# An expert layer's helper work: a gate's exponential later in ScalarE's queue, raw words loaded two parts ahead, all scaled output copies on ScalarE

## Chip, cores and metric

One core of a Trainium2 chip runs the whole program. The metric is device time in microseconds (us), from the median of three runs; lower is better.

## What is computed

Three layers follow one another: a gated recurrent attention (4 x 8 heads, 768 steps, 40 wide), a top-1 mixture of 8 experts over 3072 tokens of width 320, and a dense layer with a rational activation. The change lies in the second and in the preparation of the third:

```
logits = xn @ en.T / tau
expert_idx = argmax(logits); probs = softmax(logits)
gate_w = probs[token, expert_idx]
for e in range(8):
    h = maximum(x[mask] @ w1[e], 0)
    out[mask] = gate_w[mask, None] * (h @ w2[e])
...
h = x @ w_in                     # third layer, 320 -> 2048
g = P(h) / Q(h); return g @ w_out
```

`w_in` and `w_out` are handed over as raw 8-byte words, which the kernel turns into pairs of fp32 parts (a high and a low one).

## The kernel before

Every fp32 product is made of three products of shorter operands: each matrix is split into a high part (`h1`, `h2`, `hh`, `xh`) and a remainder (`l1`, `l2`, `hl`, `xl`). ScalarE writes the high part, VectorE or GpSimd the remainder by a subtraction.

The expert stage is a hand-ordered loop of 64 blocks `n`, eight (`fb` 0 to 7) for each of eight experts `e`. The order in which the loop writes instructions is the order of every engine's queue. A block does the following.

- `gemm1(n)` multiplies 128 columns of `w1[e]` with the expert's tokens (TensorE, L228, into one of two banks `ph`); ScalarE writes `hh` (L1454) and VectorE `hl` (L1455). A bank is free again, for block n+2, when `hl` has been read from it.
- `gemm2(n - 2)` multiplies `hh` and `hl` with `w2` (TensorE, L1469 to L1471) into the banks `yb0` to `yb3`, one for each 128 tokens, over the eight blocks of the expert. After the last of them `y_store` copies every bank, times the gate of its token, to `ysb`: banks 0 and 2 on ScalarE (L1487), 1 and 3 on VectorE (L1483). GpSimd writes the row numbers (L1478) and sends each part out with an indirect DMA (`y_scatter`, L129). The next expert's first `gemm2` writes the same banks and so waits for these copies.
- `w_hi` and `w_lo` split the weights of an expert that comes later: one ScalarE copy (L183 in even blocks, L185 in odd ones), and two GpSimd subtractions (L192 or L196).
- `x_prep` (blocks `fb` 4 to 6) transposes the next expert's tokens; `x_load` (`fb` 0) fetches the tokens of the expert after that with indirect DMAs on GpSimd (L1421).
- Two generators are stepped in turn. `gates` makes the gates of the next expert, started in its predecessor's last block, four steps to a block: 17 small VectorE steps (a maximum L1049, a square root L1773 to L1784, a difference L1052, L1054, a reciprocal, a product L1058), then the exponential on ScalarE (L1060), then three VectorE steps (L1062 to L1066). `dbl` turns the raw words of the third layer into high and low parts: 32 parts of eight steps each, an absolute value on ScalarE (`ct`, L1371), six steps on VectorE (L1373 to L1391), and a copy to `winh` (L1394) or two stores to DRAM (L1397, L1398). Six of its steps fall into a block of the experts 1 to 4, three from expert 5 on.

`dbl_load(i)` (L1347) fetches the raw words of part i with DMAs in SyncE's queue (L1351, L1352 or L1355). Its tile `raw` has two buffers, and part i + 1 is fetched after the first step of part i. The same queue carries the experts' weights (L162 to L168) and the stores of the `dbl` parts.

The third layer's first steps (`s3_step`) are interleaved with the last five blocks, so the stage ends gradually.

Of the kernel before, what the change touches and what calls it, by code (L numbers as in the profile page):

```python
# [11 lines left out]
I32 = mybir.dt.int32  # L12
U32 = mybir.dt.uint32
AF = mybir.ActivationFunctionType
ALU = mybir.AluOpType
# [6 lines left out]
def kernel(  # L22
# [17 lines left out]
    nc = tc.nc  # L40
    B, HD, S = qT.shape
    NT, DM = out.shape
    NE, _, FE = w1.shape
# [52 lines left out]
    head = const.tile([128, NE * JS, XI], F32, name="head")  # L96
# [944 lines left out]
    nc.vector.tensor_reduce(out=midl, in_=mall, axis=AX.X, op=ALU.add)  # L1041
    nc.vector.tensor_copy(xid[:, 1:, :], midl[:, 1:, :])

    def gates(pool, g, hd, tag):

        n = g.shape[1]
        sq, lg = hd[:, :, 0], hd[:, :, 1:]
        nrm, ta, tb, mx = (pool.tile([128, n], F32, name=v + tag, bufs=1) for v in ("nrm", "ta", "tb", "mx"))
        nc.vector.tensor_reduce(out=mx, in_=lg, axis=AX.X, op=ALU.max)  # L1049
        yield  # L1050
        yield from sqrt_steps(nc, nrm, sq, ta, tb)
        nc.vector.tensor_tensor(out=lg, in0=lg, in1=mx.unsqueeze(2).broadcast_to([128, n, NE]), op=ALU.subtract)  # L1052
        yield
        nc.vector.tensor_scalar(out=nrm, in0=nrm, scalar1=1e-6, scalar2=None, op0=ALU.add)  # L1054
        yield
        nc.vector.reciprocal(out=nrm, in_=nrm)
        yield
        nc.vector.tensor_tensor(out=lg, in0=lg, in1=nrm.unsqueeze(2).broadcast_to([128, n, NE]), op=ALU.mult)  # L1058
        yield
        nc.scalar.activation(out=lg, in_=lg, func=AF.Exp)  # L1060
        yield
        nc.vector.tensor_reduce(out=g, in_=lg, axis=AX.X, op=ALU.add)  # L1062
        yield
        nc.vector.tensor_scalar(out=g, in0=g, scalar1=1e-9, scalar2=None, op0=ALU.add)
        yield
        nc.vector.reciprocal(out=g, in_=g)  # L1066
        yield
# [265 lines left out]
    with ExitStack() as mctx:  # L1333
# [9 lines left out]


        def dbl_load(i):
            raw = mp.tile([128, 3 * 128, 2], I32, name="raw", bufs=2)
            if i < 16:  # L1347
                cs = slice(i * 128, (i + 1) * 128)
                rv = raw.rearrange("p (k f) t -> p k f t", k=3)
                for k in range(2):  # L1350
                    nc.sync.dma_start(out=rv[:, k], in_=win32[k * 128:(k + 1) * 128, cs, :])  # L1351
                    nc.sync.dma_start(out=rv[64 * k:64 * k + 64, 2], in_=win32[256:320, cs, :])  # L1352
            else:
                f0 = (i - 16) * 128
                nc.sync.dma_start(  # L1355
                    out=raw[:, 0:DM, :].rearrange("p f t -> p (f t)"), in_=wout32[f0:f0 + 128, :]
                )
            sx["raw", i] = raw
# [42 lines left out]
        def dbl():  # L1401
            for i in range(ND):
                for k, _ in enumerate(dbl_split(i)):
                    if k == 0 and i + 1 < ND:
                        dbl_load(i + 1)
                    yield

        def slots(k):
# [66 lines left out]
        def y_store(e, js):  # L1475
            j0, j1 = js[0], js[-1] + 1
            ysb = mp.tile([128, 4, YR], F32, name="ysb", bufs=1)
            nc.gpsimd.tensor_copy(ysb[:, j0:j1, 0].bitcast(I32), xid[:, e, j0:j1])  # L1478
            for j in js:
                r = rows(e, j)  # L1480
                gj = gate[:r, JS * e + j:JS * e + j + 1]
                if j % 2:
                    nc.vector.tensor_scalar(  # L1483
                        out=ysb[:r, j, 1:], in0=sr["yb"][j][:r, 0:DM], scalar1=gj, scalar2=None, op0=ALU.mult
                    )
                else:
                    nc.scalar.activation(out=ysb[:r, j, 1:], in_=sr["yb"][j][:r, 0:DM], func=AF.Copy, scale=gj)  # L1487
                if e < NE - 1:
                    y_scatter(e, j, ysb)
            sx["ysb"] = ysb  # L1490
# [46 lines left out]
                x_prep(0, kk, (*phs, pt0)[kk][:, NP:])  # L1537

        coef_load()
        dbl_load(0)  # L1540
        dbls = dbl()

        with tc.tile_pool(name="ov", bufs=1) as ov, tc.tile_pool(name="ovp", bufs=1, space=PSUM) as ovp:
# [104 lines left out]
        for n in range(NB + LAG2):  # L1648
            e, fb = divmod(n, NFB)
            qq, half = divmod(n, 2)  # L1650
            if n < NB:
                gemm1(n)
            if n >= LAG2:
                gemm2(n - LAG2)

            if n == NB - 12:
                y_load(0)
            for kk in range(3):
                if n == XPN[kk]:
                    x_prep(NE, kk)  # L1660
            if n == S3N[0]:
                banks(tctx, "h", 3)
            if n == NB:
                banks(hctx, "s", 2, side="right")
                sr["S"] = sr["s"].rearrange("p a b -> p (a b)")[:, 0:2 * TG].rearrange("p (a b) -> p a b", a=2)
            if n in S3N:
                s3_step(S3N.index(n))
            for p, at in enumerate((NB - 6, NB - 6, NB - 4, NB - 2, NB, NB + 1)):
                if n == at:
                    wout_load(p)  # L1670
            if n >= NB:
                continue
            if half == 0 and 5 < qq + 4 < 4 * NE:
                w_load(qq + 4)
            if fb == 0 and 1 < e + 1 < NE:
                x_load(e + 1)
            if n == 5:
                y_store(0, range(NP // 128))
            if n == 2:

                b4 = [v.unsqueeze(2).broadcast_to([128, NE, JS]) for v in (within, start)]
                t4 = mp.tile([128, NE, JS], F32, name="t4", bufs=1)
                nc.vector.tensor_tensor(out=t4, in0=slot, in1=b4[0], op=ALU.is_ge)
                nc.vector.scalar_tensor_tensor(
                    out=t4, in0=t4, scalar=2.0**20, in1=slot, op0=ALU.mult, op1=ALU.add
                )
                nc.vector.tensor_tensor(out=yrow, in0=t4, in1=b4[1], op=ALU.add)
            if 4 <= fb <= 6 and e + 1 < NE:
                x_prep(e + 1, fb - 4)
            if 3 < qq + 3 < 4 * NE:  # L1690
                w_hi(qq + 3, half)
                for i in range(2):
                    w_lo(qq + 3, 2 * half + i, nc.vector if half and n < 10 else nc.gpsimd)


            if n == 1 or fb == NFB - 1 and e + 1 < NE:
                g = 0 if n == 1 else e + 1
                gs = slice(g * JS, g * JS + slots(g).stop)
                gsteps = gates(mp, gate[:, gs], head[:, gs, :], "g")
            a, b, c = (W0 * min(max(v - NFB, 0), 4 * NFB) + W1 * max(min(v, DE) - 5 * NFB, 0) for v in (n, n + 1, NB))  # L1700
            nd, ng = b * ND * NS // c - a * ND * NS // c, (4 if n > 5 else 6) if n else 0
            for i in range(max(nd, ng)):
                if i < ng:
                    next(gsteps, None)
                if i < nd:
                    next(dbls)
# [128 lines left out]
```

## Time and profile before

| | |
|---|---|
| median of 3 runs | 845.56 us (842.04 to 846.34) |
| the profiled execution | 845.91 us |
| its span, first to last instruction | 844.2 us |
| busy over the span: TensorE / VectorE / ScalarE / GpSimd | 91% / 89% / 58% / 71% |
| instructions: VectorE, ScalarE | 1421, 839 |
| the expert loop | from about 225 us to about 475 us |

Busy time is what an engine's instructions take from start to end, so an instruction that is held up after its start counts as busy. A wait is idle time before an instruction, put down to what ended it. In the tables PE is TensorE, DVE VectorE, ACT ScalarE, POOL GpSimd and SPq the queue of SyncE.

### The profile page before, as it was taken

The numbers are of one execution on the slowest core, as the hardware profiler recorded it, in microseconds if no ns is written. First come the engines' busy times: TensorE is split into PE (matmuls) and PEld (weight loads), VectorE is DVE, ScalarE is ACT, GpSimd is POOL, SyncE is SP. The second block draws the span as 40 slices with busy tenths as digits, with TensorE's granted clock in tenths as the row PEclk, the third lists the DMA queues.
The fourth block names the chain that finished last, engine by engine and source line by source line (L and its number), as shares of the span: only waits on it lengthen the run. The fifth ranks groups of instructions, "written<-read, shape, count | busy, mean of one in ns | idle before, by whom it ended". The sixth has DMA issues, their size and how long they took to land.

```text
span 844.2 us, 14447 instructions
## 1 busy us (share of the span) xinstructions
PE 769.7 (91%) x4724; PEld 712.9 (84%) x4724; DVE 749.7 (89%) x1421; ACT 488.6 (58%) x839; POOL 595.4 (71%) x595
## 2 busy tenths in 40 slices
PE   8988988978798897988889899999999999999994
PEld 5877776768787777888789799999999999999993
DVE  7999999998589999999898988888889888988882
ACT  5243333333346454434544887878787877787772
POOL 6654343464565857767874578998989898989883
PEclk6899999998999999999999999999999999999998
DMA  8998788643465656577677303000101010000000
GB/s 207 257 241 236 224 238 223 195 130 98 130 190 161 197 158 197 171 217 218 192 223 223 102 16 110 17 32 16 32 15 33 9 40 9 17 1 24 1 24 24
DMA packets 86964, 102.41 MB, mean 121 GB/s; under 512 B 7915, under 2 KB 79219, under 8 KB 86880
## 3 DMA queue, kind: packets, MB, share of 16 engines
q1 hardware_dynamic: 82976, 88.63, 36.9%
q0 software_dynamic: 3904, 12.77, 4.7%
q8 instruction: 39, 0.64, 0.3%
q14 instruction: 45, 0.37, 0.2%
HBM read 84.01 MB, written 17.93 MB: 121 GB/s over the span
## 4 chain that ended last, share of the span: by engine, by line
PE 47%; DVE 12%; DMA 4%; issue 3%; ACT 3%; POOL 2%; SPq 1%; POOLq 0%; ACTq 0%; DVEq 0%
PE h L228 20%; PE yb L1300 6%; PE yb L1298 6%; PE yb L1299 6%; PE ph L228 4%; DMA r<-in_w 2%; DVE hl L1455 2%; DMA raw<-in_w_out 2%; DVE head L1058 1%; DVE nrmg L1784 1%; PE yb L1469 1%; PE yb L1470 1%; PE yb L1471 1%; PE h L1101 1%; DVE ct L1375 1%
## 5 line engine op out<-in xcount | busy, mean ns | idle before, releaser
L1238 POOL TENSOR_TENSOR U<-U,A 128x768 f32<-128x768 f32 (+1 forms) x65 | 119.3, 1835 | 28.6 <-ACT U L1230 23.9
L1300 PE MATMUL yb<-wo,gl 128*128 128x320 f32 x384 | 119.5, 311 | 1.8 <-POOL gl L1284 1.8
L1284 POOL TENSOR_TENSOR gl<-P,gh 128x768 fp32r<-128x768 f32 x63 | 117.8, 1870 | 3.7 <-ACT gh L1281 3.0
L1298 PE MATMUL yb<-wo,gh 128*128 128x320 f32 x384 | 119.2, 310 | 1.2 <-ACT gh L1281 1.2
L1299 PE MATMUL yb<-wo,gh 128*128 128x320 f32 x384 | 119.0, 310 | 0.0
L192 POOL TENSOR_TENSOR l<-r,h 128x384 fp32r<-128x384 f32 x64 | 67.1, 1072 | 56.5 <-ACT h L183 48.3
L1214 ACT ACTIVATE P<-h,coef 128x768 f32<-128x768 f32 (+1 forms) x65 | 64.0, 985 | 72.0 <-PE h L228 72.0
L228 PE MATMUL h<-xh,winh 128*128 128x384 f32 x256 | 90.5, 353 | 3.9 <-DVE P L1247 3.8
L228 PE MATMUL h<-xh,winl 128*128 128x384 f32 x256 | 86.6, 338 | 0.0
L228 PE MATMUL h<-xl,winh 128*128 128x384 f32 x256 | 86.4, 338 | 0.0
L1242 DVE TENSOR_TENSOR P<-P,h 128x768 f32<-128x768 f32 (+1 forms) x65 | 61.2, 941 | 27.8 <-ACT A L1222 23.1
L1469 PE MATMUL yb<-h,hh 128*128 128x320 f32 (+1 forms) x216 | 69.1, 320 | 10.1 <-DVE ysb L1483 8.5
L228 PE MATMUL ph<-xh,h 128*128 128x256 f32 (+4 forms) x152 | 56.2, 370 | 21.2 <-DVE hl L1455 16.9
L1300 PEld LDWEIGHTS yb<-wo,gl 128*128 128x128 f32 x384 | 72.5, 189 | 2.6 <-POOL gl L1284 2.6
L1298 PEld LDWEIGHTS yb<-wo,gh 128*128 128x128 f32 x384 | 72.6, 189 | 1.5 <-ACT gh L1281 1.5
L1299 PEld LDWEIGHTS yb<-wo,gh 128*128 128x128 f32 x384 | 72.5, 189 | 0.0
L1232 POOL TENSOR_SCALAR U<-A,coef 128x768 f32<-128x768 f32 x56 | 55.1, 984 | 21.3 <-ACT A L1222 20.8
L1470 PE MATMUL yb<-l,hh 128*128 128x320 f32 (+1 forms) x216 | 68.1, 315 | 0.0
L1471 PE MATMUL yb<-h,hl 128*128 128x320 f32 (+1 forms) x216 | 68.0, 315 | 0.0
L1247 DVE SCALAR_TENSOR_TENSOR P<-P,coef,h 128x768 f32<-128x768 f32 (+1 forms) x65 | 65.2, 1003 | 2.3
L1273 DVE SCALAR_TENSOR_TENSOR P<-P,coef,s 128x768 f32<-128x768 f32 (+1 forms) x62 | 62.0, 1000 | 1.7
L1265 DVE SCALAR_TENSOR_TENSOR U<-U,s 128x768 f32<-128x768 f32 (+1 forms) x62 | 58.0, 935 | 4.4 <-ACT s L1261 4.3
(693 smaller groups left out, 2386.2 us busy)
## 6 DMA issues: line engine op xcount, KB each, us to landing
fb<-fz_d SPq DMA_DIRECT2D x22, 512.0 KB
r<-in_w SPq DMA_DIRECT2D x32, 320.0 KB
r<-in_w SPq DMA_DIRECT2D x32, 256.0 KB
raw<-in_w_out SPq DMA_DIRECT2D x16, 320.0 KB
r<-in_w SPq DMA_DIRECT2D x64, 64.0 KB
raw<-in_w_in SPq DMA_DIRECT2D x32, 128.0 KB
x_rows<-xt SPq DMA_DIRECT2D x24, 164.5 KB
xt<-y_sorted SPq DMA_DIRECT2D x8, 481.5 KB
```

Of the source, the lines that this page charges most:

```text
L192: eng.tensor_tensor(out=l1[:, :, sl], in0=r1[:, :, sl], in1=h1[:, :, sl].bitcast(F32), op=ALU.subtract)
L228: mms = [nc.tensor.matmul(ps, lhsT=a, rhs=b, start=(i == 0), stop=(i == 7)) for i, (a, b) in enumerate(seq)]
L1214: r = nc.scalar.activation(out=part("P", m, i), in_=part("ph", m, i), func=AF.Identity, scale=coef[:, 3:4], bias=coef[:, 2:3])
L1238: eng.tensor_tensor(out=U, in0=U, in1=part("A", m, i), op=ALU.mult)
L1247: r = nc.vector.scalar_tensor_tensor(out=P, in0=P, scalar=coef[:, 1:2], in1=part("ph", m, i), op0=ALU.add, op1=ALU.mult)
L1284: eng.tensor_tensor(out=part("gl", m, i), in0=part("P", m, i), in1=part("gh", m, i).bitcast(F32), op=ALU.subtract)
L1298: nc.tensor.matmul(y, lhsT=gh[:, i, t], rhs=wh, start=first, stop=False)
L1299: nc.tensor.matmul(y, lhsT=gh[:, i, t], rhs=wl, start=False, stop=False)
L1300: nc.tensor.matmul(y, lhsT=gl[:, i, t], rhs=wh, start=False, stop=last)
L1469: nc.tensor.matmul(y, lhsT=hh[:, js], rhs=h2[:, half, :], start=(fb == 0), stop=False)
L1470: nc.tensor.matmul(y, lhsT=hh[:, js], rhs=l2[:, half, :], start=False, stop=False)
L1471: nc.tensor.matmul(y, lhsT=hl[:, js], rhs=h2[:, half, :], start=False, stop=(fb == NFB - 1))
```

## The change

Three edits. `gates` takes a number of extra turns before the exponential: four for the gates of experts 1 to 7, none for expert 0. `raw` gets a third buffer, parts 0 and 1 are fetched at the start, and the first step of part i is followed by the fetch of part i + 2. In `y_store` ScalarE makes all the scaled copies.

```diff
-    def gates(pool, g, hd, tag):
+    def gates(pool, g, hd, tag, turns=0):
...
         nc.vector.tensor_tensor(out=lg, in0=lg, in1=nrm.unsqueeze(2).broadcast_to([128, n, NE]), op=ALU.mult)
-        yield
+
+        for _ in range(1 + turns):
+            yield
         nc.scalar.activation(out=lg, in_=lg, func=AF.Exp)
...
-            raw = mp.tile([128, 3 * 128, 2], I32, name="raw", bufs=2)
+            raw = mp.tile([128, 3 * 128, 2], I32, name="raw", bufs=3)
...
-                    if k == 0 and i + 1 < ND:
-                        dbl_load(i + 1)
+                    if k == 0 and i + 2 < ND:
+                        dbl_load(i + 2)
...
-                if j % 2:
-                    nc.vector.tensor_scalar(
-                        out=ysb[:r, j, 1:], in0=sr["yb"][j][:r, 0:DM], scalar1=gj, scalar2=None, op0=ALU.mult
-                    )
-                else:
-                    nc.scalar.activation(out=ysb[:r, j, 1:], in_=sr["yb"][j][:r, 0:DM], func=AF.Copy, scale=gj)
+                nc.scalar.activation(out=ysb[:r, j, 1:], in_=sr["yb"][j][:r, 0:DM], func=AF.Copy, scale=gj)
...
-        dbl_load(0)
+        for i in range(2):
+            dbl_load(i)
...
-                gsteps = gates(mp, gate[:, gs], head[:, gs, :], "g")
+                gsteps = gates(mp, gate[:, gs], head[:, gs, :], "g", 4 if g else 0)
```

ScalarE's queue where expert 4's outputs are copied (`y_store`) and on to the exponential of the gates of expert 6, before; lines of the changed kernel are up to three off (L1060 there is L1062, L1487 is L1484).

```order
L1454 ACTIVATE hh_6337<-ph1_119 128x384
L1487 ACTIVATE ysb_6353<-yb0_113,gate_85 128x320
L1487 ACTIVATE ysb_6353<-yb2_4256,gate_85 128x320
L185 ACTIVATE h2_6309<-r2_6187 128x640
L1454 ACTIVATE hh_6389<-ph0_118 128x384
L183 ACTIVATE h1_6408<-r1_6292 128x768
L1454 ACTIVATE hh_6431<-ph1_119 128x384
L185 ACTIVATE h2_6409<-r2_6296 128x640
L1060 ACTIVATE head_84<-head_84 128x3x8
L1371 ACTIVATE ct_6451<-raw_6326 128x320
L1454 ACTIVATE hh_6468<-ph0_118 128x384
```

Now, the same place:

```order
L1456 ACTIVATE hh_6339<-ph1_119 128x384
L1484 ACTIVATE ysb_6355<-yb0_113,gate_85 128x320
L1484 ACTIVATE ysb_6355<-yb1_114,gate_85 128x320
L1484 ACTIVATE ysb_6355<-yb2_4261,gate_85 128x320
L1484 ACTIVATE ysb_6355<-yb3_4265,gate_85 64x320
L185 ACTIVATE h2_6311<-r2_6189 128x640
L1456 ACTIVATE hh_6391<-ph0_118 128x384
L183 ACTIVATE h1_6410<-r1_6294 128x768
L1456 ACTIVATE hh_6433<-ph1_119 128x384
L185 ACTIVATE h2_6411<-r2_6298 128x640
L1373 ACTIVATE ct_6452<-raw_6250 128x320
L1456 ACTIVATE hh_6467<-ph0_118 128x384
```

Two copies have become four, and the exponential is gone from its place between a weight copy (L185) and an absolute value. It stands one block later in the changed queue:

```order
L1456 ACTIVATE hh_6467<-ph0_118 128x384
L1098 ACTIVATE xt4_6300<-xt4_6300 128x3x64
L1079 ACTIVATE xh0_6491<-pt_6486 128x352
L183 ACTIVATE h1_6495<-r1_6404 128x768
L1062 ACTIVATE head_84<-head_84 128x3x8
L1456 ACTIVATE hh_6516<-ph1_119 128x384
```

So one `hh`, one token copy and one weight copy of an even block (L183) now come ahead of it; the `hh` and the weight copy of the next block still come behind.

SyncE's queue in expert 4, at the end of two parts of `w_out` (`ct` and `lo3` are the parts that are stored, `raw` the words that are fetched), before:

```order
L1397 DMA wouth_d_2550<-ct_5810 128x320
L1398 DMA woutl_d_2551<-lo3_5882 128x320
L1355 DMA raw_5892<-in_w_out 128x640
L1397 DMA wouth_d_2550<-ct_5888 128x320
L1398 DMA woutl_d_2551<-lo3_5948 128x320
L1355 DMA raw_5957<-in_w_out 128x640
```

Now:

```order
L1399 DMA wouth_d_2550<-ct_5812 128x320
L1400 DMA woutl_d_2551<-lo3_5884 128x320
L1357 DMA raw_5894<-in_w_out 128x640
L1399 DMA wouth_d_2550<-ct_5890 128x320
L1400 DMA woutl_d_2551<-lo3_5950 128x320
L1357 DMA raw_5959<-in_w_out 128x640
```

The places of loads and stores are the same. What a load brings has moved: `raw_5957` before is read two parts after the one that is stored ahead of it, `raw_5959` now three parts after.

## Rows read from the trace of the kernel before

**Rows 1.** The page's first line.
```profile
span 844.2 us, 14447 instructions
```

**Rows 2.** Busy time by stretch: microseconds from the span's start, length, then each engine.
```profile
core 0: us, PE busy (x) PEld busy (x) DVE busy (x) ACT busy (x) POOL busy (x), PEclk, DMA share, GB/s
...
255.00:455.00 200.00, 175.16 (x996) 161.10 (x997) 190.63 (x385) 94.50 (x189) 141.53 (x148) 0.97 0.64 191
455.00:475.00 20.00, 20.00 (x126) 19.69 (x124) 15.00 (x25) 14.44 (x20) 4.85 (x3) 1.00 0.67 207
```

**Rows 3.** Waits of VectorE from 255 to 455 us: total, times, longest.
```profile
DVE ct L1373 <- ACT ct L1371: 3.6, 5, 1.5
DVE hl L1455 <- ACT hh L1454: 2.4, 3, 1.3
DVE gate L1062 <- ACT head L1060: 0.7, 2, 0.4
DVE xr L1082 <- ACT xr L1077: 0.6, 2, 0.4
```

**Rows 4.** Waits of ScalarE from 225 to 475 us.
```profile
ACT head L1060 <- DVE head L1058: 36.7, 8, 6.2
ACT ct L1371 <- DMA raw<-in_w_out: 21.3, 9, 5.1
...
ACT ct L1371 <- DMA raw<-in_w_in: 14.3, 7, 6.6
```

**Rows 5.** Waits of TensorE from 225 to 475 us.
```profile
PE ph L228 <- DVE hl L1455: 16.9, 14, 2.8
PE yb L1469 <- DVE ysb L1483: 8.5, 4, 3.0
```

**Rows 6.** The line of VectorE's scaled copies: nanoseconds least, median, most.
```profile
L1483 DVE TENSOR_SCALAR ysb<-yb,gate x13: 531/541/546, 237.8 to 475.0; 128x320 f32<-128x320 f32 x11, 64x320 f32<-64x320 f32 x2
```

**Rows 7.** The line of ScalarE's scaled copies.
```profile
L1487 ACT ACTIVATE ysb<-yb,gate x16: 512/524/530, 237.6 to 475.8; 128x320 f32<-128x320 f32 x14, 96x320 f32<-96x320 f32 x2
```

**Rows 8.** Timeline from 289 us: start, length, instruction, idle before and its releaser.
```profile
289.43 0.97 POOL L129 DMA_INDIRECT y_sorted<-ysb,yrow  x1 [0.30 <-DMA raw<-in_w_in]
...
289.99 5.82 DVE L1052 TENSOR_TENSOR head<-head,mxg 128x32 f32<-128x32 f32 x1
...
290.43 1.73 POOL L196 TENSOR_TENSOR l<-r,h 128x320 fp32r<-128x320 f32 x2
...
292.11 1.98 POOL L192 TENSOR_TENSOR l<-r,h 128x384 fp32r<-128x384 f32 x2
...
294.06 1.70 POOL L196 TENSOR_TENSOR l<-r,h 128x320 fp32r<-128x320 f32 x2
...
297.92 0.50 PE L228 MATMUL ph<-xh,h 128*128 128x512 f32 x1 [1.92 <-DVE hl L1455]
...
298.05 0.23 ACT L1060 ACTIVATE head<-head 128x32 f32<-128x32 f32 x1 [5.51 <-DVE head L1058]
```

**Rows 9.** The chain that ended last, merged: start, length, what.
```profile
425.41 5.25 DVE head L1058
```

**Rows 10.** Timeline of VectorE from 406 us.
```profile
406.70 1.15 DVE L1378 TENSOR_SCALAR st__6452<-raw 128x320 int32<-128x320 int32 x1
407.88 1.19 DVE L1380 SCALAR_TENSOR_TENSOR vt<-raw,st__6452 128x320 f32<-128x320 uint32 x1
```

**Rows 11.** Timeline from 357 to 370 us.
```profile
357.11 0.38 SPq L1355 DMA_DIRECT2D raw<-in_w_out  x1
...
361.58 0.49 ACT L1371 ACTIVATE ct<-raw 128x320 f32<-128x320 f32 x1 [5.07 <-DMA raw<-in_w_out]
...
362.10 0.33 DVE L1373 TENSOR_SCALAR ct<-ct 128x320 int32<-128x320 int32 x1 [0.86 <-ACT ct L1371]
...
369.05 0.31 DVE L1378 TENSOR_SCALAR st__5954<-raw 128x320 int32<-128x320 int32 x1
...
369.39 0.49 DVE L1380 SCALAR_TENSOR_TENSOR vt<-raw,st__5954 128x320 f32<-128x320 uint32 x1
```

## The prediction, made before the changed kernel ran

> **What bounds the kernel now.** I read the table by stretch first, then the waits of each engine in the expert loop, then the timeline where the long waits fall. The table says which engine is full where the change is made: from 255 to 455 us VectorE is busy 190.6 of 200 us, TensorE 175.2, GpSimd 141.5, ScalarE 94.5 [rows 2]. VectorE is therefore the chain of these 200 us. What it loses to waits there is short: 3.6 us for `ct`, 2.4 for `hh`, 0.7 for the exponential and 0.6 for a token copy [rows 3]. The last twenty microseconds of the stage belong to TensorE (20.0 of 20.0 [rows 2]). TensorE's own long waits are for VectorE: 16.9 us for `hl` and 8.5 us for a scaled copy [rows 5]. They follow from VectorE being late. TensorE has 24.8 us of idle time in the 200, so it does not cap a gain of up to that size.
>
> ScalarE's waits look larger than they are worth: 36.7 us for VectorE's product before the exponential, 35.6 us (21.3 and 14.3) for raw words [rows 4]. ScalarE is half idle anyway, so of these 72.3 us only what makes VectorE wait counts.
>
> The timeline shows what VectorE's busy time is made of. At 289.99 us a difference of 128 x 32 elements takes 5.82 us [rows 8]. It starts while GpSimd is in the last scatter of an expert (289.43 to 290.40), and it ends when six GpSimd subtractions in a row, piled up behind the four scatters, are done (1.73, 1.98 and 1.70 us a pair, to 295.76). Behind it TensorE waits 1.92 us for `hl` and ScalarE 5.51 us at the exponential. One such hold follows the scatters of each of five experts, from 290 us to the last at 425.4, where 5.25 us of it lie on the chain [rows 8, 9].
>
> **The change part by part.** The sum is made against the profiled execution, 845.9 us, whose span is 844.2 [rows 1] with 1.7 us around it; it stands 0.35 us above the median of 845.56.
>
> *Scaled copies.* VectorE loses 13 instructions of 541 ns [rows 6]: 7.0 us. I count all of it, because nearly all 13 lie where VectorE is the chain. ScalarE gains 13 of 524 ns [rows 7], 6.8 us, and has 105 of the 200 us free. Four copies in a row take 2.1 us there. They follow the last `gemm2` bank by bank, and TensorE needs the first bank again only after a whole `gemm1`, the second a little later, so this should cost nothing; if that cover were missing (ScalarE late in its queue), TensorE would wait for the banks as it does now, 8.5 us in all [rows 5], though for the other engine. Behind the copies on ScalarE stand a weight copy, a `ct` and the next `hh`; GpSimd's scatters wait for the copies and come a little earlier. With those 8.5 us gone TensorE runs ahead sooner and then waits for `hl`: I book nothing for it.
>
> *Raw words.* Before, the words are issued at 357.11 us, ScalarE starts on them at 361.58 after waiting 5.07, and VectorE waits 0.86 for the result [rows 11]. One part further ahead the words land a part's time earlier, several microseconds, so I take ScalarE's 35.6 us of waiting as gone. The queue of SyncE keeps its order and its blocking points (the third buffer is freed by the same read that freed the second). On the chain this is worth at most VectorE's waits for `ct` and `hh` in rows 3, 6.0 us, some of which have other causes.
>
> *Exponential.* At most the 0.7 us of the gate wait [rows 3]; the three VectorE steps after it move by one block and stay the same. The two last edits together: between 0 and 6.7 us. I take half, 3.4, because a VectorE that idles less will meet a busy GpSimd instead in part of that time.
>
> *The hold.* This is the unknown. ScalarE at the exponential is stuck while VectorE is held, so GpSimd gets no new weights to subtract, and that ends the row of six. In the changed queue the next `hh` and a weight copy of an even block stand ahead of the exponential. Then one more pair of L192 can join the row and hold VectorE 1.98 us longer [rows 8]. Met later, the pair costs VectorE less: two instructions take 1.15 and 1.19 us there [rows 10] where they take 0.31 and 0.49 undisturbed [rows 11], 1.54 in all. The net is 1.98 - 1.54 = 0.44 for each hold; for five holds 2.2 us, which I take. The ends: one pair less in each (the scatters come earlier, with less piled up), minus 2.2; one pair more with nothing saved later, 5 x 2.0 = plus 10.
>
> The Trainium skill speaks of this resource in "SBUF — State Buffer", section "Who interferes with whom": VectorE with two SBUF inputs and a GpSimd instruction that reads SBUF exclude each other, and "whoever issues first gets the shared pair for the whole instruction". Taken literally a wait would last one GpSimd instruction, about a microsecond, and a longer row would cost nothing. The 5.82 us over six instructions speak against that reading; by it the 2.2 us would fall out of the sum below, leaving 835.5.
>
> The sum: -7.0 - 3.4 + 2.2 = -8.2, so 837.7 against the profiled execution and **837.4 us** against the median. The rivals' times are against the median.
>
> **The rivals.**
>
> *Refilled.* VectorE's 7 us come back as time in which it meets GpSimd, because what the two share is nearly full: GpSimd is busy 141.5 of the 200 us [rows 2], and the copies that leave read a bank of TensorE's results, and all took 531 to 546 ns [rows 6], so they were never held. Then only -3.4 + 2.2 is left: 844.4 us, no change to be told. For it: VectorE's slow instructions are slow because of GpSimd. Against: GpSimd's work stays the same, and the copies stand where GpSimd sends its scatters, not where it subtracts.
>
> *Longer holds, slower.* ScalarE, no longer stuck, feeds two more pairs into each of the five rows, 1.98 and 1.73 us [rows 8], and VectorE meets no less afterwards: 5 x 3.7 = 18.6. Against a gain of 10.4 that is +8.2: 853.8 us. It decides from 10.4 / 5 = 2.1 us a hold, one pair with nothing saved. For it: nothing but ScalarE's stop and the landing of weights ends a row. Against: in the changed order ScalarE stops at the exponential again after one pair, and TensorE cannot go on without `hl`, nor then `hh`.
>
> *Everything returns.* The holds shrink by a pair and all of VectorE's waits go: -7.0 - 6.7 - 2.2 = -15.9, 829.7 us. For it: TensorE's idle time allows it. Against: the hold is as long as GpSimd's backlog.
>
> The change may also not do what it says: raw words could still come late, because SyncE's queue stands at a store when they should be issued. Then up to 3.4 of the sum is missing, 840.8 us, which the forecast's own range holds.
>
> **How the numbers follow.** Forecast 0.50, with its own range 832 to 843; refilled 0.25; longer holds 0.12; everything returns 0.13. About 0.5%, 4.2 us, is what a measurement of this kernel can tell from no change: faster is below 841.3, slower above 849.8. Nearly all of the forecast and all of the last rival are faster, 0.61; refilled and the upper edge of the forecast make the middle, 0.25; longer holds and some holds with a pair for nothing (845.6 - 7.0 + 10 = 848.6) make 0.14. The range runs from 831, which leaves out half of "everything returns", to 849, the end where a pair is added for nothing and no wait is gained.
>
> **What would show it.** Right: no scaled copy on VectorE and 13 more on ScalarE at 0.52 us; ScalarE's waits for raw words near zero; TensorE's waits for a scaled copy under 2 us; a sum of VectorE's busy time lower by about 5 us; the holds after the scatters between 5.3 and 7.7 us, with six or eight subtractions in them; TensorE's waits for `hl` longer one by one. The stage then ends about 8 us sooner, and the third layer keeps its length. Wrong: holds of nine microseconds and TensorE's waits for `hl` growing past 25 us (longer holds); VectorE's busy time unchanged with more slow instructions of about 1.1 us (refilled); or a wait of TensorE for ScalarE's copies in place of the 8.5 us.

## The result and the profile after

The changed kernel is slower: the ratio to the kernel before is 1.0057, with a 95% interval of 1.0037 to 1.0076. Every ratio in this document is taken over fast runs alone (a slow run is longer as a whole), so this one is not the quotient of the medians below, and two of the twelve runs of `e2_no_raw` (923 and 4094 us) do not count in its ratio.

| | before | changed |
|---|---|---|
| median of 18 runs each | 845.33 us (838.70 to 857.25) | 849.06 us (845.62 to 854.98) |
| the profiled execution, its span | 845.9, 844.2 us | 850.5, 847.9 us |
| a second profiled execution, its span | 843.15, 841.0 us | 849.12, 847.4 us |
| the loop in the two profiles | 250.8, 246.5 us | 252.5, 252.1 us |
| VectorE busy in the loop | 230.75, 226.97 us | 228.00, 228.88 us |
| VectorE idle in the loop | 20.05, 19.5 us | 24.5, 23.2 us |

The loop is counted from the first `hh` to the third layer's first `gh`. The page of the changed kernel, its first lines:

```profile
span 847.9 us, 14441 instructions
...
PE 776.3 (92%) x4724; PEld 723.1 (85%) x4724; DVE 747.4 (88%) x1408; ACT 495.3 (58%) x852; POOL 588.8 (69%) x595
```

The 13 instructions have left VectorE (1421 to 1408) and come to ScalarE (839 to 852). Busy time by stretch, changed kernel; the first line is the loop, the others answer to [rows 2]:

```profile
core 0: us, PE busy (x) PEld busy (x) DVE busy (x) ACT busy (x) POOL busy (x), PEclk, DMA share, GB/s
228.00:480.50 252.50, 226.78 (x1300) 212.61 (x1300) 228.00 (x462) 130.92 (x251) 162.65 (x172) 0.94 0.62 186
255.00:455.00 200.00, 175.40 (x985) 163.53 (x984) 186.60 (x372) 99.01 (x196) 137.86 (x147) 0.93 0.64 191
455.00:475.00 20.00, 20.00 (x126) 20.00 (x126) 14.82 (x27) 10.84 (x17) 6.04 (x6) 1.00 0.52 163
```

The loop of the kernel before, in its two profiles:

```profile
225.40:476.20 250.80, 223.74 (x1299) 206.88 (x1298) 230.75 (x474) 124.07 (x239) 164.81 (x172) 0.97 0.63 188
```

```profile
225.50:472.00 246.50, 224.17 (x1298) 207.23 (x1298) 226.97 (x474) 124.77 (x238) 163.54 (x172) 0.97 0.63 192
```

Of the 13 copies 12 lie in the loop (474 and 462 VectorE instructions), 12 x 541 ns = 6.5 us. Yet VectorE's busy time there fell by only 0.4 us in the mean of two profiles (228.9 to 228.4), and its idle time grew by 4.1 (19.8 to 23.9). Together that is the loop's +3.7 us (248.65 to 252.3). Two profiles of one kernel differ by up to 4.3 us in the length of the loop and 3.8 us in VectorE's busy time, so each of these means is good to some 2 us, and no difference of that size is shown by one profile. The loop also begins 2.5 us later (228.0 and 227.9 against 225.4 and 225.5), after instructions that the edits don't touch. Over all kernels below this start lies between 223.4 and 228.2 us without relation to their edits. The time after the loop fell by 1.1 us.

The waits that the edits aimed at are gone. ScalarE from 225 to 475 us, to lay beside [rows 4]:

```profile
ACT hh L1456 <- PE ph L228: 42.7, 34, 6.3
ACT winh L1396 <- DVE ct L1377: 23.9, 8, 6.2
...
ACT head L1062 <- DVE head L1058: 5.8, 3, 3.0
```

The wait at the exponential fell from 36.7 to 5.8 us, and no wait for raw words is left in the view. ScalarE gained little by it: it now stands at `hh` and `winh` instead. VectorE from 255 to 455 us, beside [rows 3]:

```profile
DVE xr L1084 <- ACT xr L1079: 3.4, 2, 2.4
DVE xl L1084 <- ACT xh L1079: 2.3, 2, 1.2
DVE hl L1457 <- ACT hh L1456: 2.2, 2, 1.1
DVE ct L1375 <- ACT ct L1373: 1.9, 3, 0.8
```

The wait for `ct` halved, the gate's is gone, and 5.7 us for ScalarE's token copies (L1079) stand where 0.6 stood. TensorE from 225 to 475 us, beside [rows 5]:

```profile
PE ph L228 <- DVE hl L1457: 25.5, 11, 4.6
```

The 8.5 us for scaled copies are gone; the wait for `hl` grew by 8.6 us (16.9 to 25.5) in fewer and longer stops. In the second profiles it is 12.7 us before and 26.1 changed.

**A hold that grew.** A *row* is a run of GpSimd subtractions one right behind the other. A *hold* is a VectorE instruction that started before or in a row and does not end until the row does. Timeline of the changed kernel behind the scatters of one expert:

```profile
425.53 0.98 POOL L129 DMA_INDIRECT y_sorted<-ysb,yrow  x1 [0.30 <-PE yb L1472]
425.55 0.19 DVE L1058 TENSOR_TENSOR head<-head,nrmg 128x24 f32<-128x24 f32 x1
426.29 9.25 DVE L1375 TENSOR_SCALAR ct<-ct 128x320 int32<-128x320 int32 x1 [0.55 <-ACT ct L1373]
426.52 1.71 POOL L196 TENSOR_TENSOR l<-r,h 128x320 fp32r<-128x320 f32 x2
428.19 1.98 POOL L192 TENSOR_TENSOR l<-r,h 128x384 fp32r<-128x384 f32 x2
429.63 0.21 ACT L1062 ACTIVATE head<-head 128x24 f32<-128x24 f32 x1
430.13 1.69 POOL L196 TENSOR_TENSOR l<-r,h 128x320 fp32r<-128x320 f32 x2
431.79 1.94 POOL L192 TENSOR_TENSOR l<-r,h 128x384 fp32r<-128x384 f32 x2
431.83 0.73 ACT L185 ACTIVATE h<-r 128x640 fp32r<-128x640 f32 x1
433.69 1.66 POOL L196 TENSOR_TENSOR l<-r,h 128x320 fp32r<-128x320 f32 x2
435.47 0.51 DVE L1457 SCALAR_TENSOR_TENSOR hl<-ph,hh 128x352 fp32r<-128x352 f32 x1
436.03 0.66 PE L228 MATMUL ph<-xh,h 128*128 128x352 f32 x1 [4.60 <-DVE hl L1457]
438.84 0.47 ACT L1456 ACTIVATE hh<-ph 128x352 fp32r<-128x352 f32 x1 [6.28 <-PE ph L228]
```

A `ct` step starts during the scatter and takes 9.25 us: ten subtractions (five lines of two) instead of the six of [rows 8]. VectorE was already past the product (425.55), so the exponential at 429.63 did not wait, and ScalarE went on to the weight copy at 431.83. That fed the fifth pair at 433.69. ScalarE stopped only at an `hh`, behind a TensorE that stood for `hl`.

A hold can also start inside a row. In the changed kernel the fourth row is ten subtractions long too (400.05 to 408.94 us). VectorE there:

```profile
400.72 0.56 DVE L1457 SCALAR_TENSOR_TENSOR hl<-ph,hh 128x384 fp32r<-128x384 f32 x1 [1.10 <-ACT hh L1456]
402.33 0.53 DVE L1084 TENSOR_TENSOR xl<-pt,xh 128x352 fp32r<-128x352 f32 x1 [1.05 <-ACT xh L1079]
402.77 6.52 DVE L1377 SCALAR_TENSOR_TENSOR ct<-raw,ct 128x320 int32<-128x320 int32 x1
```

The two that read a bank of TensorE's results (`ph`, `pt`) pass amid the subtractions in 0.56 and 0.53 us. The one behind them, which reads none, is held for the seven subtractions that are left. The five holds after scatters, as subtractions that the held instruction meets and its microseconds:

| kernel | the five holds, subtractions met/us | sum, us |
|---|---|---|
| before | 6/5.8, 6/5.7, 6/5.5, 6/5.7, 6/5.3 | 28.0 |
| before, second profile | 6/5.8, 6/5.9, 6/5.7, 5/4.3, 6/5.2 | 26.9 |
| changed | 6/5.8, 8/7.1, 6/5.0, 7/6.5, 10/9.3 | 33.7 |
| changed, second profile | 6/5.8, 8/7.1, 6/5.7, 7/6.5, 8/7.6 | 32.7 |

The rows themselves are of six in all ten cases before, and of 6, 8, 6, 10, 10 and 6, 8, 6, 10, 8 in the two profiles of the changed kernel.

The granted clock around that hold, changed kernel:

```profile
431.80:435.20 3.40, 0.00 (x0) 0.00 (x0) 3.40 (x1) 0.76 (x2) 3.40 (x5) 1.00 0.99 304
435.20:438.60 3.40, 2.57 (x9) 2.57 (x10) 3.40 (x12) 0.00 (x0) 0.40 (x2) 0.52 0.71 210
438.60:442.00 3.40, 3.40 (x15) 3.36 (x14) 1.22 (x3) 0.70 (x2) 0.00 (x0) 0.50 0.36 107
```

TensorE did nothing from 431.8 to 435.2, and then ran at 1.2 GHz until 442; the kernel before has 1.00 in all three stretches. From 255 to 455 us the changed kernel has 27 and 24 us at 1.2 GHz in its two profiles, the kernel before 14 in both.

### The profile page after: what moved, and what is told of

The parts are those of the page before. It is cut to its first block, busy times and chain, and to the rows that moved or that the text cites. A ratio compares the mean times of both kernels' runs of the same rounds, so it can differ in the third digit from the quotient of the medians.

```text
span 847.9 us, 14441 instructions
## 1 busy us (share of the span) xinstructions
PE 776.3 (92%) x4724; PEld 723.1 (85%) x4724; DVE 747.4 (88%) x1408; ACT 495.3 (58%) x852; POOL 588.8 (69%) x595
## 4 chain that ended last, share of the span: by engine, by line
PE 49%; DVE 14%; issue 3%; ACT 3%; DMA 2%; POOL 1%; POOLq 0%; SPq 0%; DVEq 0%; ACTq 0%
PE h L228 20%; PE yb L1302 6%; PE yb L1300 6%; PE yb L1301 6%; PE ph L228 5%; DVE ct L1377 2%; DVE nrmg L1782 2%; DVE hl L1457 2%; DVE vt L1382 1%; PE yb L1471 1%; PE yb L1472 1%; PE yb L1473 1%; DVE head L1058 1%; PE h L1103 1%; DVE ct L1375 1%
## 5 line engine op out<-in xcount | busy, mean ns | idle before, releaser
L192 POOL TENSOR_TENSOR l<-r,h 128x384 fp32r<-128x384 f32 x64 | 65.4, 1045 | 48.6 <-ACT h L183 48.5
L228 PE MATMUL ph<-xh,h 128*128 128x256 f32 (+4 forms) x152 | 58.6, 386 | 30.4 <-DVE hl L1457 25.5
L1244 DVE TENSOR_TENSOR P<-P,h 128x768 f32<-128x768 f32 (+1 forms) x65 | 61.2, 942 | 28.6 <-ACT A L1224 23.9
L196 POOL TENSOR_TENSOR l<-r,h 128x320 fp32r<-128x320 f32 x56 | 51.1, 935 | 23.9 <-ACT h L185 23.8
```

Source lines behind the costliest of these rows:

```text
L192: eng.tensor_tensor(out=l1[:, :, sl], in0=r1[:, :, sl], in1=h1[:, :, sl].bitcast(F32), op=ALU.subtract)
L228: mms = [nc.tensor.matmul(ps, lhsT=a, rhs=b, start=(i == 0), stop=(i == 7)) for i, (a, b) in enumerate(seq)]
```

## The experiments

### Which edit does it

Three kernels each lack one edit, three have one alone. Against the changed kernel ("..." marks arguments and lines left out):

```diff
 e1_no_exp, the exponential at its old place
-                gsteps = gates(mp, gate[:, gs], head[:, gs, :], "g", 4 if g else 0)
+                gsteps = gates(mp, gate[:, gs], head[:, gs, :], "g")
 e2_no_raw
-            raw = mp.tile([128, 3 * 128, 2], I32, name="raw", bufs=3)
+            raw = mp.tile([128, 3 * 128, 2], I32, name="raw", bufs=2)
-                        dbl_load(i + 2)
+                        dbl_load(i + 1)
...
-        for i in range(2):
-            dbl_load(i)
+        dbl_load(0)
 e3_no_copies
-                nc.scalar.activation(out=ysb[:r, j, 1:], ...)
+                if j % 2:
+                    nc.vector.tensor_scalar(out=ysb[:r, j, 1:], ...)
+                else:
+                    nc.scalar.activation(out=ysb[:r, j, 1:], ...)
```

`e1_no_exp`, expected:

> The change without its first edit: the exponential stays at its old place, raw words and scaled copies as changed. Theory 1 (the later exponential frees ScalarE while VectorE is held, so GpSimd's rows of subtractions after the scatters grow from six to eight or ten and the holds from 5.7 us to 6.8 to 8.9): holds back at six subtractions and at most 5.8 us, ratio to before 0.985 to 0.995. Theory 2 (the raw words ahead do it, since ScalarE's waits for them had paced GpSimd): holds stay at 7 to 9 us, ratio 1.003 to 1.008. Theory 3 (the copies on ScalarE do it: scatters earlier, TensorE ahead and then stopped longer at a time): as theory 2.

`e2_no_raw`, expected:

> The change without its second edit: raw words one part ahead with two buffers, exponential and copies as changed. Theory 1: holds stay as long as in the changed kernel (up to 8.9 us) unless ScalarE's waits for raw words happen to fall there, ratio 1.000 to 1.008. Theory 2: holds back at 5.8 us at most, ratio 0.985 to 0.995. Theory 3: ratio 1.003 to 1.008.

`e3_no_copies`, expected:

> The change without its third edit: banks 1 and 3 are copied on VectorE again. Theory 1: holds stay long and VectorE has its 7 us back on top, ratio 1.008 to 1.016. Theory 2: the same. Theory 3: TensorE's waits for scaled copies come back (about 8 us) but its long stops for hl shrink to 2 us, ratio 0.995 to 1.002.

The reverse of these pieces, applied to the kernel before, gives the edits alone: `e4_exp_alone` has the four turns, `e8_copies_alone` the copies, `e11_raw_alone` the raw words:

```diff
 e4_exp_alone
-                gsteps = gates(mp, gate[:, gs], head[:, gs, :], "g")
+                gsteps = gates(mp, gate[:, gs], head[:, gs, :], "g", 4 if g else 0)
 e8_copies_alone
-                if j % 2:
+                if False:
 e11_raw_alone
-            raw = mp.tile([128, 3 * 128, 2], I32, name="raw", bufs=2)
+            raw = mp.tile([128, 3 * 128, 2], I32, name="raw", bufs=3)
-                        dbl_load(i + 1)
+                        dbl_load(i + 2)
...
-        dbl_load(0)
+        for i in range(2):
+            dbl_load(i)
```

`e4_exp_alone`, expected:

> The first edit alone: exponential four turns later, all else as before. Theory 1: holds of eight or more subtractions, 6.8 us and more, ratio 1.003 to 1.012. Theories 2 and 3: holds as before (5.3 to 5.8 us), ratio 0.997 to 1.002, since ScalarE then stops at the raw words instead.

`e8_copies_alone`, expected:

> The third edit alone: all scaled copies on ScalarE, exponential and raw words as before. Theory 4 (each edit that leaves ScalarE fewer waits feeds GpSimd longer rows; this one leaves ScalarE's two big waits in place): holds stay at six subtractions, ratio 0.990 to 0.998. Theory 3 (copies on ScalarE make TensorE stop longer at a time): ratio 1.002 to 1.008.

`e11_raw_alone`, expected:

> The second edit alone: raw words two parts ahead. Theory 4: ScalarE still stops at the exponential, which ends the row at six subtractions while VectorE is held ahead of it; where VectorE is held behind it, the row grows to eight or more. Ratio 0.998 to 1.006. Theory 2: 1.003 to 1.008 with holds of 7 us or more in at least three of the five experts.

| kernel | ratio to before, 95% interval | the five holds, subtractions met/us |
|---|---|---|
| changed (all three) | 1.0057 [1.0037, 1.0076] | 6/5.8, 8/7.1, 6/5.0, 7/6.5, 10/9.3 |
| e1: raw + copies | 1.0030 [0.9998, 1.0061] | 6/6.1, 6/5.2, 6/6.2, 10/8.9, 10/9.4 |
| e2: exponential + copies | 1.0033 [0.9999, 1.0067] | 6/5.8, 7/5.9, a short one, 10/8.9, 9/8.0 |
| e3: exponential + raw | 1.0030 [0.9998, 1.0061] | 6/5.8, 6/5.9, 6/5.9, 8/7.2, 9/8.0 |
| e4: exponential alone | 1.0078 [1.0047, 1.0110] | 6/5.8, 6/5.9, 6/5.6, 8/7.2, 9/7.7 |
| e8: copies alone | 1.0030 [0.9999, 1.0062] | 6/6.1, 6/4.6, 6/5.0, 9/8.1, 10/9.4 |
| e11: raw words alone | 0.9980 [0.9949, 1.0011] | 6/5.8, 6/5.9, 6/5.9, 6/4.9, 6/5.2 |

No single edit is the culprit, and none of theories 1 to 3 fits all of these ratios. The raw words alone leave the rows of six and cost nothing that can be told. The exponential and the copies each lengthen rows by themselves. The exponential alone is slower; the copies alone show no gain. That the copies lengthen rows was not expected, since the exponential keeps its place. Timeline of `e8_copies_alone`:

```profile
426.70 0.17 DVE L1058 TENSOR_TENSOR head<-head,nrmg 128x24 f32<-128x24 f32 x1
426.97 0.23 ACT L1060 ACTIVATE head<-head 128x24 f32<-128x24 f32 x1 [1.20 <-DVE head L1058]
427.86 9.43 DVE L1064 TENSOR_SCALAR gate<-gate 128x3 f32<-128x3 f32 x1
433.71 0.74 ACT L185 ACTIVATE h<-r 128x640 fp32r<-128x640 f32 x1 [1.47 <-DMA r<-in_w]
440.58 0.46 ACT L1454 ACTIVATE hh<-ph 128x352 fp32r<-128x352 f32 x1 [6.13 <-PE ph L228]
```

VectorE, rid of two copies per expert, is already past the product (426.70) when it is held, now at a step of three elements a row (L1064). The exponential waited only 1.20 us and ScalarE went on copying weights (433.71). In both profiles of the kernel before, all ten holds begin at the product (L1058) or at a step ahead of it, so ScalarE stood 4.2 to 6.2 us at the exponential and the row ended after six. That wait was a brake on GpSimd. An edit can release it in two ways: move the exponential behind more weight copies, or let VectorE get past the product before the hold.

The rows of the other runs with the scatters and subtractions in their old order bear this out. With the exponential at its old place (both profiles before, e1, e8, e11 and e6 below), 25 holds at the product or ahead of it all have rows of six. The five behind it, two in e1, two in e8 and one in e6, all have rows of ten. With the late exponential (both profiles of the changed kernel, e2, e3, e4 and e5 below), 13 holds ahead of the product have rows of six, seven at it rows of eight, and nine behind it rows of ten; e2 has no hold after one expert. So the exponential is not the only brake. In e4 the first row still ends at six without any wait there, because ScalarE stands 1.7 us before an `hh` and 1.4 us before a token copy and copies the next weights late; GpSimd waits 1.6 us for them. In e6, the kernel before with small GpSimd writes added, the exponential waited only 0.51 us:

```profile
424.91 0.22 ACT L1061 ACTIVATE head<-head 128x24 f32<-128x24 f32 x1 [0.51 <-DVE head L1059]
426.04 8.88 DVE L1374 TENSOR_SCALAR ct<-ct 128x320 int32<-128x320 int32 x1 [0.69 <-ACT ct L1372]
```

### Are the two profiles typical?

`e12_before_again` and `e15_changed_again` are the kernel before and the changed one, profiled once more; an empty line at the end of the file is all that differs (in e15 also a branch that is never taken):

```diff
+
```

`e12_before_again`, expected:

> The kernel before once more, for a second profile of it. If the difference between the two kernels' profiles is the edits', rows of six subtractions, holds of 5.3 to 5.8 us and half-speed stretches of 3.4 us come again; if it is chance between executions, rows of eight to ten appear here too.

`e15_changed_again`, expected:

> The changed kernel once more, for a second profile. If rows of eight to ten subtractions are the change's, they come again in at least two of the five experts, with TensorE's stops for hl of 3 us and more after them; if they were chance, rows of six.

They took 843.15 and 849.12 us. Their rows, idle time and time at 1.2 GHz are in the first section: the long rows come again in the changed kernel, and only rows of six before. The start of the loop repeats to 0.1 us for each kernel, so it belongs to the kernel and not to the run, though not to these edits.

### What ends a hold

If VectorE is let through between two GpSimd instructions, a GpSimd instruction that only writes, put ahead of every subtraction, should end it. `e5_break_changed` does this to the changed kernel, `e6_break_before` to the kernel before (`brk` is 128 x 1):

```diff
                 for i in range(2):
+                    if not (half and n < 10):
+                        nc.gpsimd.memset(brk, 0.0)
                     w_lo(qq + 3, 2 * half + i, nc.vector if half and n < 10 else nc.gpsimd)
```

`e5_break_changed`, expected:

> The changed kernel, with a GpSimd memset of one column (it writes and reads nothing) ahead of each GpSimd subtraction of the expert loop. Theory 4 (the gain is eaten by holds: a VectorE instruction that starts in a scatter or load stays held until GpSimd pauses reading, however many subtractions stand in the row): each memset lets the held instruction through, no hold over 2.2 us, ratio to before 0.975 to 0.992. Rival (a memset is no pause, or the holds cost nothing in the end because TensorE or GpSimd is the bound): holds of 6 to 11 us stay, or they go and the ratio stays 1.000 to 1.015 by GpSimd's added work.

`e6_break_before`, expected:

> The kernel before, with the same memsets. Theory 4: the five holds of 5.3 to 5.8 us go, ratio 0.985 to 0.997, a smaller gain than in the changed kernel, since ScalarE still waits at the exponential and the raw words. Rival: ratio 1.000 to 1.010.

Measured: 1.0096 [1.0069, 1.0124] and 1.0079 [1.0047, 1.0110], both slower. Timeline of `e5_break_changed`:

```profile
290.13 0.97 POOL L129 DMA_INDIRECT y_sorted<-ysb,yrow  x1 [0.30 <-issue]
290.49 6.38 DVE L1380 TENSOR_SCALAR st__5101<-raw 128x384 int32<-128x384 int32 x1
291.10 0.11 POOL L1697 MEMSET brk<- 128x1 f32 x1
291.15 0.89 POOL L196 TENSOR_TENSOR l<-r,h 128x320 fp32r<-128x320 f32 x1
...
295.76 0.85 POOL L196 TENSOR_TENSOR l<-r,h 128x320 fp32r<-128x320 f32 x1
296.56 0.09 POOL L1697 MEMSET brk<- 128x1 f32 x1
```

The held instruction lasts until the row of six is over, across the memsets between them. A write-only instruction does not end this hold; the end of the row does. The memsets also add instructions to GpSimd, so the two ratios say nothing on what the holds cost.

Not every VectorE instruction that meets a row is held to its end. GpSimd in the kernel before, around the two VectorE instructions of [rows 10]:

```profile
406.57 2.14 POOL L192 TENSOR_TENSOR l<-r,h 128x384 fp32r<-128x384 f32 x2 [2.54 <-ACT h L183]
408.67 1.96 POOL L196 TENSOR_TENSOR l<-r,h 128x320 fp32r<-128x320 f32 x2
```

These subtractions too stand one right behind the other, and yet VectorE's two instructions end after 1.15 and 1.19 us, each after about one subtraction. What makes the difference no run here shows.

### Shorter rows

Two ways to shorten a row were tried ("..." marks arguments and lines left out). *Pace*: from block 10 on, the subtractions of block n wait for `hl` of block n. *Spread*: the scatters of an expert go out one per block, behind the block's subtractions; *ahead* is the same with the scatter ahead of them.

```diff
 pace: e7_pace_changed, e14_spread_pace, e17_ahead_pace
-                    w_lo(...)
+                    lo = w_lo(...)
+                    if n >= 10:
+                        tc.add_manual_dep(lo.ins, sx["hl", n].ins.name, ..., reason="pace")
 spread: e9_spread_changed, e10_spread_before, e13_spread_no_exp, e14_spread_pace
-                    y_scatter(e, j, ysb)
+                    later.append((e, j, ysb))
...
                     w_lo(...)
+            if later:
+                y_scatter(*later.pop(0))
 ahead: e16_spread_ahead, e17_ahead_pace
+            if later:
+                y_scatter(*later.pop(0))
             if 3 < qq + 3 < 4 * NE:
                 w_hi(qq + 3, half)
```

`e7_pace_changed`, expected:

> The changed kernel, with GpSimd's subtractions of block n waiting for VectorE's hl of block n, from block 10 on, so that GpSimd cannot go on with blocks that VectorE has not reached. Theory 4: rows of at most six subtractions, holds of at most 5.8 us as before, with the 7 us of VectorE's copies kept: ratio 0.985 to 0.997. Rival (the long holds are a result, not the cause): ratio 1.002 to 1.010.

`e9_spread_changed`, expected:

> The changed kernel, with an expert's four scatters sent one in each of four blocks, behind that block's two subtractions, instead of four in a row. Theory 4 (what eats the gain is the row of subtractions piled up behind four scatters, during which VectorE stands still and TensorE with it): no row over four subtractions, no hold over 4 us, TensorE's stops for hl under 2.5 us, ratio to before 0.980 to 0.993. Rival (refilled: VectorE and GpSimd share a resource that is nearly full, and it makes no difference how the meeting is dealt out): the long holds go, VectorE's time above its undisturbed durations stays at 75 to 83 us, ratio 1.000 to 1.008.

`e10_spread_before`, expected:

> The kernel before with the scatters spread in the same way. Theory 4: ratio 0.988 to 0.998 (holds of 5.7 us go, TensorE's waits for scaled copies on VectorE stay), so the three edits are worth 0.3 to 1% on top of it. Rival: ratio 0.998 to 1.006, and the changed kernel with spread scatters not faster than this one.

`e13_spread_no_exp` is e1 with spread, `e14_spread_pace` the changed kernel with both. Expected:

> Scatters spread, raw words ahead and copies on ScalarE, but the exponential at its old place. Theory 4 (the later exponential costs only because it lets the row behind four scatters grow): without such a row the place of the exponential hardly matters, ratio to before 0.994 to 1.001, within 0.4% of the run with spread scatters and the later exponential (0.997). Rival (the later exponential costs by something else, such as ScalarE's own queue): this kernel clearly faster than 0.997, 0.985 to 0.992.

> The changed kernel with spread scatters and with GpSimd's subtractions of block n waiting for VectorE's hl of block n. Theory 4: rows of at most four subtractions, holds under 4.6 us, and a ratio of 0.988 to 0.998, at least as fast as with spread scatters alone. Rival (pacing takes from GpSimd what spreading gave): 1.000 to 1.006.

`e16_spread_ahead` is the changed kernel with ahead, `e17_ahead_pace` with ahead and pace. Expected:

> The changed kernel with one scatter in each of four blocks, now ahead of the block's two subtractions, so that a scatter (and the pause at its issue) stands between any two pairs behind the loads. Theory 4: no row over two subtractions from the loads to the last scatter, no hold over 3 us there, ratio to before 0.986 to 0.997. Rival (the length of the rows is not what counts, and the gain of the spread kernel came from elsewhere): ratio 0.998 to 1.006 in spite of shorter holds.

> The same with GpSimd's subtractions of block n waiting for VectorE's hl of block n, from block 10 on. Theory 4: holds as in the kernel without the wait, ratio 0.986 to 0.999. Rival: 1.000 to 1.006, since GpSimd is late for what it needs when it waits twice.

| kernel | ratio to before | longest hold, subtractions met/us | loop, us | VectorE busy in it, us |
|---|---|---|---|---|
| changed, two profiles | 1.0057 [1.0037, 1.0076] | 10/9.3 | 252.5, 252.1 | 228.00, 228.88 |
| e7: changed, pace | 1.0014 [0.9992, 1.0036] | 8/7.5 | 248.5 | 231.93 |
| e9: changed, spread | 0.9972 [0.9942, 1.0003] | 4/4.8 | 248.1 | 223.78 |
| e14: changed, spread and pace | 0.9979 [0.9953, 1.0005] | 4/4.7 | 248.7 | 227.59 |
| e16: changed, ahead | 1.0000 [0.9968, 1.0033] | 6/5.7, the others 2 | 248.7 | 228.63 |
| e17: changed, ahead and pace | 0.9968 [0.9937, 1.0000] | 4/4.6, the others 2 | 248.3 | 231.25 |
| e13: raw + copies, spread | 1.0012 [0.9983, 1.0041] | 4/4.8 | 249.8 | 224.76 |
| e10: before, spread | 1.0067 [1.0035, 1.0098] | 4/4.7 | 253.6 | 227.08 |

All five versions of the changed kernel with GpSimd's backlog limited are faster than it, each with an interval below the 1.0037 where its own begins. Part of that can come from the start of the loop, which is 1.8 to 4.3 us earlier in all of them but e9. But the loop itself is shorter in all five, 248.1 to 248.7 us against 252.1 and 252.5. So GpSimd's unlimited backlog has a part in the loss.

That it is the length of the rows by which they do it is not shown. Against it stands e7, where the longest row is still eight and VectorE is busier than in the changed kernel; its loop is shorter because VectorE idles 16.6 us instead of 23.9. Against it stands e16 as well: its ratio is the one that its rival expected, and theory 4 asked for 0.997 or less. e7 and e9 also fell short of what theory 4 expected of them.

Nor does VectorE's busy time decide. In the five versions it runs from 223.8 to 231.9 us, and the loop stays within 0.6 us. What bounds these loops at 248 us was not tried. The loop in `e9_spread_changed`:

```profile
228.00:476.10 248.10, 224.90 (x1301) 209.70 (x1301) 223.78 (x462) 130.24 (x252) 166.93 (x172) 0.96 0.64 190
```

Here VectorE's busy time is lower: 223.78 us against a mean of 228.9 before, 5.1 less. Not all of that is the copies: e10, which spreads the scatters and moves no copy, has 227.08, so 3.3 us lie between the two, one profile each. VectorE's idle time in e9, 248.10 - 223.78 = 24.3 us, stays as high as in the changed kernel, and takes 4.5 of the 5.1 back.

On the kernel before, spreading shortens the holds too and costs 0.67%. TensorE's waits there, `e10_spread_before`:

```profile
PE yb L1469 <- DVE ysb L1485: 13.3, 4, 4.7
```

TensorE waits longer for VectorE's scaled copies (13.3 us against 8.5), and in the changed kernel there are none. That these waits are what the spreading costs here was not tried apart. With spread, dropping the late exponential turns 0.9972 into 1.0012; without it, 1.0057 into 1.0030. These intervals overlap, so a change of sign is suggested, not shown. None of the versions is shown to beat the kernel before: e9 and e17 lie 0.3% below it at the edge of their intervals.

## Why the prediction was wrong

The forecast was 837.4 us and faster. The changed kernel took 849.06, 0.06 us beyond the upper end of the range, and slower. That it came so near is luck: that end stands for one more pair in each of five rows and VectorE's waits unchanged, and three rows grew while VectorE waited longer.

*Scaled copies* (-7.0). "I count all of it, because nearly all 13 lie where VectorE is the chain": this step failed. The cost of each copy on ScalarE is as booked, the line of them in the changed kernel (least, median, most ns):

```profile
L1484 ACT ACTIVATE ysb<-yb,gate x29: 512/528/540, 240.3 to 480.1; 128x320 f32<-128x320 f32 x25, 64x320 f32<-64x320 f32 x2, 96x320 f32<-96x320 f32 x2
```

TensorE's waits for them went to nothing, as said. But VectorE's busy time in the loop fell by 0.4 us where 5 were forecast. The 12 copies went out, 6.5 us, and 5.7 us of longer holds came in. Shortening VectorE's queue also moves what it is held at when the scatters come, and in e8 that alone released the brake. The premise beneath it, "VectorE is therefore the chain of these 200 us", is not borne out either: in the five versions with a limited backlog 8 us more or less of VectorE's busy time leave the loop where it is. VectorE's 190.6 us [rows 2] contain the holds, and were no sign that a microsecond of work taken out is a microsecond won.

*Raw words and exponential* (-3.4). The waits of ScalarE fell as forecast, 35.6 to none and 36.7 to 5.8. The prediction had seen that "only what makes VectorE wait counts", but still took a gain. Of VectorE's waits those for `ct` halved, and new ones of 5.7 us for token copies took their place. ScalarE's idle time in the loop fell only from 124 to 122 us (means of two profiles); it moved to `hh` and `winh`. VectorE idled 4.1 us more instead of 3.4 less.

*The hold* (+2.2). This is the step that failed by its reasoning: "in the changed order ScalarE stops at the exponential again after one pair". At 429.63 the exponential had not waited at all, because VectorE was held behind the product. Where it was held at the product the row did grow by one pair, as booked. The prediction asked what stands ahead of the exponential in ScalarE's queue, but not what VectorE would be held at, and that decides whether ScalarE stops there. The holds grew by 5.7 us in sum (27.5 to 33.2, means of two profiles), and three rows of five by one pair or two, where 2.2 us net were booked.

*The clock*, which had no term. Against 14 us at 1.2 GHz from 255 to 455 us stand 27 and 24. In the first profiles, six stops of TensorE of 2.8 to 4.6 us stand in the loop in place of ten of 1.6 to 3.0. What it costs end to end was not measured apart. In the same stretch e14 has 7 us at 1.2 GHz, e7 and e17 14 and e9 20, but e16 has 27, as much as the changed kernel, and its loop is as short as theirs. So the clock alone is not the loss.

*The rivals.* "Longer holds, slower" named the mechanism, rows of ten and TensorE's waits for `hl` past 25 us (25.5 and 26.1), and got a chance of 0.12. Its price was too high: it put two pairs into each of five rows, 18.6 us. Three rows grew, by one, two and two pairs in the first profile and by one, two and one in the second, and the holds by 5.7 us in sum. "Refilled" named where VectorE's time went, busy time unchanged, and its 844.4 us is nearer than the forecast. The figures fit both together: VectorE saves the copies and pays for what GpSimd is fed earlier.

The Trainium skill's sentence that the holder gets the shared pair "for the whole instruction" ("SBUF — State Buffer", section "Who interferes with whom") would, taken literally, have made a longer row free. Against that stand 9.25 us over ten subtractions, at none of whose ends VectorE got in. The 1.15 and 1.19 us of [rows 10] fit it.

*Open.* What shifts the loop's start by up to 4.8 us between kernels was not tried, though 2.5 us of the 5.1 by which the spans differ (means of two profiles) enter there. Nor is it settled which wait takes back 4.5 us in e9, where holds are short, or what holds the limited loops at 248 us.

## What to carry to other kernels

A wait on a half-idle engine may be a brake: here ScalarE's stop at the exponential kept it from feeding GpSimd, whose work holds up VectorE, the full engine. Before such a wait is removed, follow what the freed engine issues next and who competes with the full engine over it, and try limiting that competitor's backlog (here by pacing its subtractions or dealing out its scatters; on the kernel before, dealing out cost 0.67%). A busy share that contains held time does not say what work taken out is worth. And when work leaves the full engine, look at which instruction it will then be at when the next long hold begins.

## What was not expected

- A held VectorE instruction was not let in between back-to-back GpSimd instructions, not even at a write-only memset of 128 x 1 between each two (6.38 us across six in e5); each hold above ended with its row. Other VectorE instructions got through after one subtraction (1.15 and 1.19 us [rows 10]).
- The held instruction's size did not set the length of the hold: a `TENSOR_SCALAR` of 128 x 3 with a single input tile took 9.43 us (e8), one of 128 x 320 integers 9.25.
- Taking out an edit that only moves loads (e2) or one that makes VectorE do less (e3) made the changed kernel no slower: the edits' effects do not add up. The exponential alone (1.0078 [1.0047, 1.0110]) costs about as much as all three together (1.0057 [1.0037, 1.0076]).
